# First chunk loaded in four-token runs over two hardware queues, scaled and turned by groups of heads, its layers taken batch by batch

The kernel runs on one core of one Trainium2 chip. The metric is the device time of the core in microseconds (us), as a median of the fast runs; less is better. Faster or slower needs 2%, with a 95% interval that lies clear of it.

## The reference

```python
def _attn_ref(q, k, v, alpha):            # each (4, 8, 768, 48): batch, head, token, dimension
    state = zeros((B, H, D, D)); y = zeros_like(q)
    for t in range(S):
        state = alpha[:, :, t, :, None] * state + einsum('bhd,bhe->bhde', k[:, :, t], v[:, :, t])
        y[:, :, t] = einsum('bhd,bhde->bhe', q[:, :, t], state)
    return y

def _moe_ref(x, w_in, w_out):             # x (3072, 384), w_in (384, 2048), w_out (2048, 384)
    h = x @ w_in
    c = sqrt(2.0 / pi)
    g = 0.5 * h * (1.0 + tanh(c * (h + 0.044715 * h * h * h)))
    return g @ w_out
# reference(): x is y with heads side by side, (4*768, 384); the result is _moe_ref(x)
```

So the work is linear attention with a decay per token, and then a feed-forward of two layers with a GELU between them. All of it is float32 at the borders.

## The kernel before

Time is cut into six chunks of 128 tokens. A chunk has two **pairs** of batches, so there are twelve pairs, 0 to 11. Pairs 0 and 1 are the first chunk, pair 2 is the first half of the second. For each pair ScalarE takes the logarithm of alpha, TensorE forms prefix sums over the tokens (a product with a triangle of ones), ScalarE takes two exponentials (of the sums and of their negatives), and VectorE scales q and k with them. TensorE turns q and k, multiplies them to scores, VectorE masks these, TensorE multiplies with v, and the result is copied and turned once more to be the input of layer 1. A state per batch is carried from chunk to chunk.

The order of the instructions on each engine is fixed when the kernel is built, by a list scheduler that works with guessed durations `W`. The loads of before run through one software queue, issued by GpSimd (POOL), but for the first alpha, which the SP queue takes:

```python
    DECAYS = {-1: (0, 1), 1: (2, 3), 2: (4,), ...}
    SPLIT = (2,)                       # pair 2 is loaded and scaled in two halves
    LOADS = ("0", "1", "in 0", "in 1", "in 2", "in 3", "out 0", "out 1", "out 2", "out 3",
             "2", "3", "4", "5", "6", "7", "8", "9", "10", "11")
    # "0" is alpha, q, k, v of pair 0; "in 0" the first quarter of w_in; "out 0" of w_out

    def load(self, n, c, i, lo=0, hi=2):          # tokens are the partitions: runs of 48 floats
    # ... cut: the tile; emit(e) opens ...
            src = self.src[n][2 * i + lo:2 * i + hi].rearrange("b h s d -> s (b h) d")[c * C:(c + 1) * C]
            (nc.sync if e == "SP" else nc.gpsimd).dma_start(u[n][:, lo:hi].rearrange("t b h d -> t (b h) d"), src)

    def fill(self, n):                            # "idle": products of zeros, meant to keep TensorE's clock up
    # ... cut ...
            for _ in range(n):
                self.nc.tensor.matmul(ps, self.zero[:, 0:self.C], self.zero, start=True, stop=True)
    # ... cut ...
        for m in range(len(self.BLOCKS)):         # the order of the layers: a block is a pair
            layer1(m)
            if m:
                for j in (0, 1) if m == 1 else (m,):
                    layer2(j)                     # block 0: quarter of w_out by quarter, over its two batches
```

Layer 2 of pairs 0 and 1 comes after layer 1 of both. Tile names in the profile: `a`, `la` alpha and its logarithm, `cum` prefix sums, `qp`, `kp` scaled q and k, `qkT` these turned, `at`, `atm` scores and masked scores, `yps` attention's output, `hT` layer 1, `gT` GELU, `acc` layer 2, `idle` the products of zeros.

## Time and profile before

| | before |
|---|---|
| time, median of 3 runs | 188.59 us (188.59 to 188.68) |
| span of the profiled run | 186.9 us |
| TensorE (PE) busy | 176.7 us, 95% |
| ScalarE (ACT) / VectorE (DVE) busy | 71% / 56% |
| products of zeros | 31, 11.2 us |
| share of the software queue, 16 DMA engines | 74.4% |

TensorE is busy nearly all the time, and where it is busy on zeros there is something to gain. That is only in the first 50 us, before it has a steady supply of work. The lines of the profile that show it are in the prediction below.

### The profile page before, as it was taken

To read this page: it belongs to the slowest core of one execution; us is meant where nothing else is said; L and a number is where in the kernel's file an instruction comes from. 1 tells how busy PE (TensorE), PEld (TensorE's weight loads), DVE (VectorE), ACT (ScalarE), POOL (GpSimd) and SP (SyncE) were. 2 spreads that over 40 slices of the span, in tenths; PEclk is the share of its full clock that TensorE was granted. 3 is DMA by queue.
4 is the path that set the end of the run, shared out by engine and by line. 5 is a ranking of instruction groups with operands and counts; after the bars stand their busy time and mean duration, and the time that the engine had idled before them with its cause. 6 is when DMAs were issued, how large, how long until landed. Compare 5 with 4: busy or idle time off the path is not lost.

```text
span 186.9 us, 4504 instructions
## 1 busy us (share of the span) xinstructions
PE 176.7 (95%) x1831; PEld 127.2 (68%) x1834; DVE 104.0 (56%) x219; ACT 131.8 (71%) x297; POOL 63.8 (34%) x67
## 2 busy tenths in 40 slices
PE   5788899999999999999999999999999999999990
PEld 1344688666687687687688778667687687786850
DVE  7268670079787597497499798696644615000000
ACT  2544889853769769859799759788789884582911
POOL 7993443796456575566552200000000000000000
PEclk9999999999999999999999999999999999999999
DMA  6999999999999999999999997153270280301111
GB/s 131 174 183 169 206 204 212 200 178 229 240 217 186 151 227 205 175 231 200 180 218 222 186 207 136 43 123 76 46 178 22 49 190 14 101 15 47 42 42 44
DMA packets 49781, 27.56 MB, mean 147 GB/s; under 512 B 39744, under 2 KB 46400, under 8 KB 49760
## 3 DMA queue, kind: packets, MB, share of 16 engines
q0 software_dynamic: 32464, 19.27, 74.4%
q1 hardware_dynamic: 17296, 8.00, 17.5%
q8 instruction: 14, 0.23, 0.6%
q14 instruction: 7, 0.06, 0.1%
HBM read 25.17 MB, written 4.72 MB: 160 GB/s over the span
## 4 chain that ended last, share of the span: by engine, by line
PE 88%; ACT 4%; DVE 3%; DMA 2%; issue 1%
PE hT L400 34%; PE acc L414 34%; PE at L327 4%; PE qkT_ps L291 4%; PE cum L254 3%; PE yps L376 2%; DMA a<-in_alpha_dram 2%; PE yps L373 2%; PE kv L344 2%; PE idle L209 2%; PE xT_ps L390 1%; DVE atm L334 1%; ACT qkT L305 1%; PE cum L256 1%; DVE qp L280 1%
## 5 line engine op out<-in xcount | busy, mean ns | idle before, releaser
L406 ACT ACTIVATE gT<-hT 128x256 bf16<-128x256 f32 x192 | 63.5, 386 | 11.0 <-PE hT L400 10.5
L400 PE MATMUL hT<-xT,w_in 128*128 128x256 bf16 x576 | 69.9, 273 | 0.3 <-ACT gT L406 0.2
L414 PE MATMUL acc<-w_out,gT 128*128 128x384 bf16 x384 | 68.6, 326 | 0.0
L400 PEld LDWEIGHTS <-w_in 128*128 128x128 bf16 x576 | 54.2, 98 | 8.6 <-issue 0.8
L414 PEld LDWEIGHTS <-gT 128*128 128x128 bf16 x384 | 35.7, 97 | 20.4
L334 DVE TENSOR_TENSOR atm<-at,ut 128x512 bf16<-128x512 f32 x48 | 31.0, 686 | 13.8 <-PE at L327 12.9
L280 DVE TENSOR_TENSOR qp<-q,b 128x768 bf16<-128x768 f32 (+1 forms) x13 | 11.6, 892 | 19.0 <-ACT b L272 16.7
L421 ACT COPY ot<-acc 128x384 f32<-128x384 f32 x17 | 8.2, 480 | 18.7 <-PE acc L414 18.5
L222 POOL DMA_DIRECT2D k<-in_k_dram x13 | 14.5, 1113 | 12.3 <-DVE kp L280 6.0
L222 POOL DMA_DIRECT2D q<-in_q_dram x13 | 14.6, 1122 | 9.5 <-DMA q<-in_q_dram 3.0
L222 POOL DMA_DIRECT2D v<-in_v_dram x13 | 14.4, 1111 | 7.3 <-DMA a<-in_alpha_dram 2.7
L222 POOL DMA_DIRECT2D a<-in_alpha_dram x12 | 13.3, 1110 | 7.8 <-DMA k<-in_k_dram 1.9
L272 ACT ACTIVATE b<-cum 128x768 bf16<-128x768 f32 (+1 forms) x13 | 9.9, 762 | 7.7 <-PE cum L256 7.6
L243 ACT ACTIVATE la<-a 128x768 f16<-128x768 f32 (+1 forms) x13 | 10.2, 793 | 3.5 <-DMA a<-in_alpha_dram 3.3
L209 PE MATMUL idle<-zero 128*128 128x512 bf16 x31 | 11.2, 483 | 1.4 <-DVE zero L596 1.2
L361 DVE TENSOR_TENSOR st<-stmp,bend 64x192 bf16<-64x192 f32 x32 | 11.3, 353 | 1.7
L200 ACT ACT_TABLE_LOAD x9 | 11.5, 1283 | 0.9 <-PEq L629 0.7
L280 DVE TENSOR_TENSOR kp<-k,binv 128x768 bf16<-128x768 f32 (+1 forms) x15 | 11.7, 792 | 0.2 <-DMA k<-in_k_dram 0.2
L359 DVE TENSOR_TENSOR stmp<-kv,st 64x192 f32<-64x192 f32 x32 | 11.3, 352 | 0.9 <-PE kv L344 0.6
L406 ACT ACT_TABLE_LOAD x9 | 11.5, 1283 | 0.2
L305 DVE COPY qkT<-qkT_ps 128x1024 bf16<-128x1024 bf16 (+1 forms) x14 | 8.8, 649 | 4.7 <-PE qkT_ps L291 4.6
L383 DVE CAST x<-yps 128x384 bf16<-128x384 f32 x12 | 6.7, 556 | 7.6 <-PE yps L376 7.5
(43 smaller groups left out, 151.3 us busy)
## 6 DMA issues: line engine op xcount, KB each, us to landing
out_dram<-ot SPq DMA_DIRECT2D x24, 192.0 KB, 3.8
q<-in_q_dram POOLq DMA_DIRECT2D x11, 384.0 KB, 13.2
k<-in_k_dram POOLq DMA_DIRECT2D x11, 384.0 KB, 13.2
a<-in_alpha_dram POOLq DMA_DIRECT2D x10, 384.0 KB, 13.0
v<-in_v_dram POOLq DMA_DIRECT2D x11, 192.0 KB, 13.0
w_in<-in_moe_w_in_dram POOLq DMA_DIRECT2D x4, 384.0 KB, 11.8
w_out<-in_moe_w_out_dram POOLq DMA_DIRECT2D x4, 384.0 KB, 15.3
a<-in_alpha_dram SPq DMA_DIRECT2D x1, 384.0 KB, 4.2
```

Of the source, the lines that this page charges most:

```text
L200: nc.scalar.add_instruction(mybir.InstLoadActFuncSet(name=nc.get_next_instruction_name(), act_func_set_id=i, engine=mybir.EngineType.Activ ...
L209: self.nc.tensor.matmul(ps, self.zero[:, 0:self.C], self.zero, start=True, stop=True)
L222: (nc.sync if e == "SP" else nc.gpsimd).dma_start(u[n][:, lo:hi].rearrange("t b h d -> t (b h) d"), src)
L243: self.nc.scalar.activation(u["la"][:, lo:hi, :, 0:self.D], u["a"][:, lo:hi], AF.Ln)
L280: self.nc.vector.tensor_tensor(u[n + "p"][:, lo:hi, :, 0:self.D], u[n][:, lo:hi], u["b" if n == "q" else "binv"][:, lo:hi], op=ALU.mult)
L305: self.copy(e)(t, u.pop(("T_ps", i, which)))
L334: self.nc.vector.tensor_tensor(u["atm", i][:, o], u["at", i][:, o], self.ut[:, None, :].to_broadcast([self.C, self.H // 2, self.C]), op=AL ...
L359: nc.vector.tensor_tensor(s[ps], acc, old[ps, :, fs], op=ALU.add)
L361: nc.vector.tensor_tensor(new[ps, :, fs], acc, u["bend"][ps, i, :, None].to_broadcast([64, H // 2, D]), op=ALU.mult)
L400: self.nc.tensor.matmul(h, self.w_in[:, j, nt * self.C:(nt + 1) * self.C], self.xT[c][:, j, lo:hi].rearrange("p g t -> p (g t)"), start=j ...
L406: return lambda e: self.nc.scalar.activation(self.gT[c % self.NG][:, nt, lo * self.C:hi * self.C], f.pop(("h", c, lo, nt)), AF.Gelu_apprx_ ...
L414: self.nc.tensor.matmul(f["acc", c, b], self.gT[c % self.NG][:, nt, b * self.C:(b + 1) * self.C], self.w_out[:, nt, :], start=nt == 0, sto ...
```

## The change

The intent is to shorten that head. Alpha, q and k of the first chunk, all four batches, are loaded with four tokens to a partition (runs of 768 B in place of 192 B), over the SP and the ScalarE hardware queues. The other loads wait until that alpha has landed. Prefix sums, exponentials, scaling and turning of the first chunk go by groups of two heads over all four batches at once. Batches 0 and 1 go singly through layer 1, layer 2 of the first chunk goes batch by batch (before, pair 0's went quarter of `w_out` by quarter over its two batches), pair 2 is loaded ahead of `w_out`, and pair 2 is no longer split. Layer 1 of the whole chunk comes ahead of its layer 2, as before. The diff, cut to its core:

```diff
-    SPLIT = (2,)
-    LOADS = ("0", "1", "in 0", "in 1", "in 2", "in 3", "out 0", "out 1", "out 2", "out 3", "2", "3", ...)
+    SPLIT = ()
+    LOADS = ("v0","v1","in 0","in 1","in 2","in 3","2","out 0","out 1","out 2","out 3","3", ...)
+    R = 4
+    ON_ACT = (("a", 2), ("a", 3), ("q", 2), ("q", 3))
@@
+    def load_first(self, n, b):
+            src = self.src[n][b, :, 0:self.C].rearrange("h (j r) d -> j h (r d)", r=R)
+            dst = self.first[n].rearrange("(j b) h r d -> b j h (r d)", b=4)[b]
+            (self.nc.sync if e == "SP" else self.nc.scalar).dma_start(dst, src)
@@
+    def cum_first(self, g, p):
+            for r in range(R):
+                for s in range(R):
+                    nc.tensor.matmul(cum[:, r * n:(r + 1) * n], self.ut_blk[s > r], la[:, s, :, 0:D],
+                                     start=s == 0, stop=s == R - 1, skip_group_check=True)
@@
+        for r in "aqk":
+            for b in range(B):
+                load([(r, "first")], "ACT" if (r, b) in self.ON_ACT else "SP", ..., self.load_first(r, b))
+        load(["gate"], "POOL", 100, 0, lambda e: self.nc.gpsimd.tensor_copy(self.gate, self.first["a"][:, 0, 0, 0:1]))
+        loads["gate"][0].deps += loads["a", "first"]
@@ (four groups of two heads; scores of any batch need all eight turned products)
+        for p in range(4):
+            ln = s.add("ln", ..., self.ln_first(g, p), loads["a", "first"], LN_EXP)
+            cum = s.add("cum", ..., self.cum_first(g, p), [ln])
+            ... two exponentials, two products, two turns with their copies ...
@@
-        for m in range(len(self.BLOCKS)):
-            layer1(m)
-            if m:
-                for j in (0, 1) if m == 1 else (m,):
-                    layer2(j)
+        layer1(0, 0, 1)
+        layer1(0, 1, 2)
+        layer1(0, 2, 4)
+        decays(2)
+        layer2(0, 0, 2)
+        decays(3)
+        layer2(0, 2, 4)
+        ...
```

The first run of zeros is guessed anew as well: ten products of zeros start after the changed set-up, where before had six. Cut above, and part of the change all the same: other guessed durations in `W` (a quarter of a weight 2000 ns for 1850, for instance), five `ot` buffers for six, and other buffers for some of the scores. They too can change the order on the engines.

## The prediction

> **What bounds the kernel now.** I read the page first (busy shares, the slices, the chain that ended last), then the same chain in order of time, then the busy times of each engine in short windows, and last the waits of the queue that issues the loads.
>
> ```profile
> PE 176.7 (95%) x1831; PEld 127.2 (68%) x1834; DVE 104.0 (56%) x219; ACT 131.8 (71%) x297; POOL 63.8 (34%) x67
> PE   5788899999999999999999999999999999999990
> PE 88%; ACT 4%; DVE 3%; DMA 2%; issue 1%
> L209 PE MATMUL idle<-zero 128*128 128x512 bf16 x31 | 11.2, 483 | 1.4 <-DVE zero L596 1.2
> ```
>
> TensorE is the bound: 176.7 us busy of 186.9, and 88% of the chain that ended last. But 11.2 us of that busy time are the "idle" matmuls on zeros, which keep its clock up while it has nothing to do, and nearly all of them lie in the first five slices. So time can be gained only in the head, before TensorE has a steady diet. The chain in order of time says where the head ends:
>
> ```profile
> 0.74 4.18 DMA a<-in_alpha_dram
> 6.83 3.01 PE idle L209 x7
> 19.50 1.65 ACT qkT L305 x3
> 22.04 1.31 PE hT L400 x12
> 27.32 6.55 PE hT L400 x60
> 33.87 2.60 PE acc L414 x16
> 50.28 1.14 PE hT L400 x9
> ```
>
> The first column is the start in us, the second the length. Layer 1 of the first chunk starts at 22.04, its layer 2 at 33.87, and layer 1 of pair 2 (the second chunk's first half) at 50.28. I call this last moment **S**. After it TensorE runs through to 182.74 with one hole of 2.25 us, at 123.04 to 125.29 (output copy, table load, first GELU). So the time is S + 136.6 us (186.9 - 50.28), plus 1.7 us between span and median time (188.59 - 186.9): **time = S + 138.3**. The change is worth what it does to S.
>
> What feeds the head are the loads, one queue that never pauses:
>
> ```profile
> 15.16 0.74 POOL L235 DMA_DIRECT2D w_out<-in_moe_w_out_dram  x1 [0.82 <-DMA q<-in_q_dram]
> 17.31 0.74 POOL L235 DMA_DIRECT2D w_out<-in_moe_w_out_dram  x1 [1.41 <-DMA k<-in_k_dram]
> 18.64 0.74 POOL L235 DMA_DIRECT2D w_out<-in_moe_w_out_dram  x1 [0.59 <-DMA v<-in_v_dram]
> DMA to landing us min/median/max: 14.8/15.3/15.6
> ```
>
> The issuer waits until an earlier load has landed, so its waits are landing times: q of pair 1 at 15.1, k at 17.3, v at 18.6. A 384 KB strip of alpha, q or k thus takes 2.15 us of wire, a v strip 1.3. The last w_out quarter was issued at 18.64 and landed 15.6 us later, at 34.2, so the eight weight quarters took (34.2 - 18.6)/8 = 1.95 us each. Check: first alpha lands at 4.92; less 2.1 of wire, 2.8 us of start; 2.8 + 6 strips x 2.15 + 2 x 1.3 + 8 x 1.95 = 33.9, against 34.2 seen.
>
> **What the skill says.** The Trainium skill, "DMA: Bandwidth & Descriptors", section Specifications: runs under 512 B do not reach line rate. Agrees: the 192 B runs of alpha give 393 KB / 2.15 us = 183 GB/s, while output stores alone in the tail (1536 B runs) move 51 GB/s at a share of 0.16 and 40 at 0.11, 320 to 360 GB/s while busy. The same page, section Queues, rings and completion order: each engine takes turns between queues packet by packet; and its Rules for kernel authors: spreading loads over issuing engines saves only issue time. The trace fits: a 192 KB store lands in 1.9 us with the engines free, but 3.8 us in the median, as it shares with the loads. So two hardware queues are no second wire, and q and k will have to share with v and weights. "TensorE: Matmul & The Clock Gate", Part 1: TensorE runs at half clock until kept busy for about 3.4 us. Agrees in kind: the first six zero matmuls of 512 columns take 2.74 us (0.46 each), three at 10.21 only 0.81 (0.27 each).
>
> **The change, part by part.**
>
> *Loads in four-token runs.* Six strips of chunk 0 (alpha, q, k of both pairs) become twelve pieces of 192 KB with runs of 4 x 48 x 4 = 768 B. At some 340 GB/s (the stores) a piece takes 0.58 us, all twelve 7.0 us against 6 x 2.15 = 12.9. The wire is 5.9 us ahead from then on. Alpha of all four batches lands at 2.8 + 4 x 0.58 = 5.1, where before half of it landed at 4.92.
>
> *Order and gate.* v and weights are issued only once alpha has landed. q and k are on the wire meanwhile, so it does not run dry. v then competes with k. If the engines share evenly from about 7 us, k lands at 11 to 14 rather than at 9.8. The order is now v, w_in, pair 2, w_out: w_in ends at 2.8 + 7.0 + 2.6 + 7.8 = 20.2 (before 26.3), pair 2 at 20.2 + 3 x 2.15 + 1.3 = 28.0 (before about 43), w_out at 28.0 + 7.8 = **35.7**, later than before's 34.2.
>
> *Decay and scaling.* All four batches at once in four groups: per group a log (0.5 us at 128x384), twenty small matmuls (16 of 96 columns at 0.043 as in kv, 4 tiny at 0.02: 0.8 us), two exponentials (0.49 each), two products (0.55), two transposed copies (about 0.5). ScalarE has 4 x 1.5 = 6 us, VectorE 4.4, and 4 us of copies fall to either: 14.4 us over two engines, so 7.2 after alpha, 12.4 at best; with k at 11 and its 2.2 us of products and the last copy, about 14. TensorE gains 2.1 us of prefix sums (3.2 for 2 x 0.53) and 0.9 us for turning k back; both lie mostly in the idle head and replace zero matmuls.
>
> *First layer by single batches.* From 14: scores 0.35, two masks 1.3 (0.65 each), y 0.2, copy 0.48, transpose 0.2, copy 0.35, and some 0.1 between each: 3.6 us, so layer 1 starts at about **17.7** instead of 22.04. A single unit costs half a pair's columns (128x128 matmuls run at about 0.055, twice as many): layer 1 of the chunk stays 10.5 us. It then waits about 1 us for the last w_in quarter. With 3 us of the other batches' scores, y, and transposes beside it, it ends at about 32 (before 33.87).
>
> *Second layer.* It now goes batch by batch, so the first batch already needs all of w_out: it stalls at each quarter and finishes at 35.7 + 0.65 = 36.35, where without the wait it would have ended at 34.6. Three batches follow, 3 x 2.6 = 7.8 us. The attention of pair 2 needs the table switch after the last GELU: 32.4 + 1.3 + log 0.85 + prefix 0.5 + two exponentials 1.6 + products 1.9 = 38.5, so nearly all its TensorE work (transposes 0.9, scores 0.66, kv 0.35, y 0.75, turns 0.34) and pair 3's prefix 0.5 fall behind the stall: 3.5 us, of which I let 0.5 hide. S = 36.35 + 7.8 + 3.0 = **47.15**, 3.1 us earlier. Time = 47.15 + 138.3 = **185.5**, 1.7% faster.
>
> After S nothing is changed in kind: pairs 2 to 11 are loaded, scaled and turned as before. The wire, 5.9 us ahead, stays ahead of a TensorE that is 3 us ahead (a pair costs 7.75 us of wire and about 13.4 of TensorE).
>
> **Rivals.**
> (a) *The load order gives it back.* If pieces run no faster than strips (1.07 us each), w_out lands at 41.6 and S is 53: time 191. The stores' rate speaks against it; for a part of it, the sharing of three queues. With pieces at 0.75 us w_out lands at 37.7 and the time is 187.5.
> (b) *k is the late one.* If v and weights take half of the engines, k lands at 14 and layer 1 starts at 20.5. The work of TensorE from there to S is 10.5 + 10.4 + 3.7 (rest of chunk 0) + 4.2 = 28.8, less 0.7 done before: S = 48.6, time 186.9. The store's 3.8 against 1.9 us speaks for it.
> (c) *The whole lead reaches the end.* If layer 1 starts by 16 and ends by 30, pair 2's attention fills the wait for w_out, and the pieces come nearer the 403 GB/s that weights reach (786 KB read in 1.95 us), 0.49 us each: S = 44.5, time 182.8. The hole at 123 us may go too, for 2 us more, or another may come: the order on each engine is fixed from guessed durations.
>
> **Range and chances.** (a) in its mild form and (b) give 187 to 188, the main line 185.5, (c) 183 or a little less. Range 182.6 to 188.4. Two per cent lie at 184.9, just under the main line; so within 2% is likeliest, 0.57; faster 0.39; slower, which needs (a) in full, 0.04.
>
> **What would show it.** Right: alpha's last landing near 5.1; first layer-1 matmul between 16.5 and 19; a wait for w_out of 1 to 3 us in the first batch of layer 2; pair 2's layer 1 near 47; from there the same 136.6 us to the end, within 1.5. Wrong: k after 14 us (then b); pieces over 0.75 us (a); no wait for w_out and S under 45 (c); or S as foretold but new holes later, where scalar work and table loads sit between the layers.

## The result

| | before | after |
|---|---|---|
| median of the same rounds | 188.63 us (188.59 to 188.68, 4 runs) | 191.10 us (190.66 to 191.76, 4 runs) |
| ratio | | 1.0134, 95% interval 1.0103 to 1.0164 |
| granted clock (share of full speed that TensorE was allowed), profiled run | over 0.9 in every slice | 0.988, 0.8 in two slices |
| span of the profiled run | 186.9 us | 189.5 us |

All runs were fast ones. A ratio is the mean time of one kernel's runs over that of the other's of the same rounds, so it is not quite the ratio of the medians quoted beside it. Executions over 1.5% slower than the fastest of the same kernel are left out of the means. The change is 1.3% slower: within 2%, but outside the range that was predicted.

The page after, the lines that answer to those of before (busy time and share and instructions of each engine; the busy tenths of TensorE in 40 slices; its granted clock in tenths; the chain that ended last, by engine):

```profile
PE 177.6 (94%) x1948; PEld 131.8 (70%) x1948; DVE 105.6 (56%) x223; ACT 134.8 (71%) x305; POOL 55.7 (29%) x59
PE   7488799999999999999989999999998999999992
PEclk9889999999999999999999999999999999999998
PE 73%; DVE 12%; DMA 6%; ACT 5%; issue 2%; SPq 1%; DVEq 0%; ACTq 0%
```

TensorE is as busy as before, but it ends the chain for 73% of the span where it was 88%, and VectorE has grown from 3% to 12%. The second and third slices (4.7 to 14.2 us) have a lower granted clock. The chain in order of time (start, length, what):

```profile
1.54 5.22 DMA a_first<-in_alpha_dram
7.43 1.29 PE cum L259 x16
8.81 1.30 PE cum L259 x16
...
11.43 0.70 PE cum L259 x16
...
18.30 0.49 PE at L444 x8
18.82 3.04 DVE atm L461 x5
...
44.29 2.53 DVE atm L461 x4
...
51.21 0.88 DVE kp L394
52.13 0.87 PE qkT_ps L405 x12
53.00 0.66 PE hT L530 x6
```

Alpha lands at 6.76, four groups of prefix sums follow one another at 1.3 us down to 0.7, and scores do not start before 18.30. From 44.29 to 52.09 the chain runs through VectorE (masks, state steps, products of pair 3). The last line is S, layer 1 of pair 2: 53.00, where before had 50.28. TensorE's own lines, in its timeline (start, length, instruction, idle time before it and what ended that):

```profile
1.20 3.81 PE L224 MATMUL idle<-zero 128*128 128x512 bf16 x10 [1.20 <-DVE zero L805]
7.43 1.29 PE L259 MATMUL cum<-la,ut_blk 128*128 128x96 f16 x16 [2.43 <-ACT la L246]
11.29 0.84 PE L259 MATMUL cum<-la,ut_blk 128*128 128x96 f16 x16
22.23 0.83 PE L530 MATMUL hT<-xT,w_in 128*128 128x128 bf16 x12
35.80 2.11 PE L549 MATMUL acc<-w_out,gT 128*128 128x384 bf16 x12
```

Layer 1 starts at 22.23 and layer 2 at 35.80. Three stages add up to S, and they say where the 2.7 us went and where the prediction went wrong:

| stage, us | before | predicted | after | after less before | after less predicted |
|---|---|---|---|---|---|
| start of layer 1 | 22.04 | 17.7 | 22.23 | +0.2 | **+4.5** |
| to the start of layer 2 | 11.83 | 14.3 | 13.57 | **+1.7** | -0.7 |
| from there to S | 16.41 | 15.15 | 17.20 | +0.8 | **+2.05** |
| S | 50.28 | 47.15 | 53.00 | +2.7 | +5.85 |
| S to the end of the span | 136.6 | 136.6 | 136.5 | -0.1 | -0.1 |

(The predicted stages are the prediction's own moments: 17.7, "ends at about 32", 47.15. Those of before are moments of the chain, as the prediction has them; in the timeline the first products of the layers are at 21.88 and 33.70, so product against product layer 1 starts 0.35 later than before, not 0.2.) The last row holds, but three things offset one another in it. Pair 3's turns, 0.87 us of TensorE's work, stand just behind S in before (at 51.43) and just ahead of it in after (at 52.13). The tail behind TensorE's last product is 0.6 us shorter (3.6 for 4.2). And TensorE idles for 1.6 us between S and its last product, where before had 0.2. The longest idle times there, in before and then two in after (TensorE's timeline; idle time and what ended it in brackets):

```profile
125.29 1.14 PE L400 MATMUL hT<-xT,w_in 128*128 128x256 bf16 x9 [0.17 <-ACT gT L406]
```

```profile
98.85 1.14 PE L530 MATMUL hT<-xT,w_in 128*128 128x256 bf16 x9 [0.69 <-ACT gT L539]
144.82 0.40 PE L444 MATMUL at<-qkT 64*128 64x128 bf16 x8 [0.59 <-DMA qkT<-kp]
```

So the "hole of 2.25 us" of the prediction, 123.04 to 125.29, was no hole: the chain leaves TensorE there, but TensorE has other products for all but 0.17 us of it.

Two further readings. The last quarter of `w_out` is issued at 23.3 and lands some 15 us later, at 38.4 rather than the predicted 35.7 (the line on `w_out` in the view of its loads):

```profile
DMA to landing us min/median/max: 15.0/15.1/15.5
```

And TensorE waits for only 0.3 us from layer 2's start to S (16.89 us busy of 17.20, zeros included). The groups of TensorE's work in that stretch (line, tile, shapes, count, then busy us and mean ns) differ in one thing that matters. Before, pair 2 alone is turned there (the row of k; that of q is like it):

```profile
L291 PE MATMUL qkT_ps<-ident,kp 128*128 128x128 bf16 x8 | 0.8, 219 | 0.0
```

After, pair 3 is turned there too, twice as many products; in the chain these are the 0.87 us just ahead of S:

```profile
L405 PE MATMUL qkT_ps<-ident,kp 128*128 128x128 bf16 x16 | 1.6, 220 | 0.1
```

### The profile page after: what moved, and what is told of

It is laid out like the page before. It is cut to its first block, busy times and chain, and to the rows that moved or that the text cites. A ratio compares the mean times of both kernels' runs of the same rounds, so it can differ in the third digit from the quotient of the medians.

```text
span 189.5 us, 4750 instructions
## 1 busy us (share of the span) xinstructions
PE 177.6 (94%) x1948; PEld 131.8 (70%) x1948; DVE 105.6 (56%) x223; ACT 134.8 (71%) x305; POOL 55.7 (29%) x59
## 4 chain that ended last, share of the span: by engine, by line
PE 73%; DVE 12%; DMA 6%; ACT 5%; issue 2%; SPq 1%; DVEq 0%; ACTq 0%
PE acc L549 28%; PE hT L530 25%; DVE atm L461 5%; PE at L444 4%; DMA qkT<-kp 3%; ACT gT L539 3%; DMA a_first<-in_alpha_dram 3%; PE qkT_ps L405 3%; PE cum L259 2%; PE yps L504 2%; PE yps L501 2%; PE cum L368 2%; DVE stmp L487 1%; PE kv L471 1%; PE xT_ps L518 1%
## 5 line engine op out<-in xcount | busy, mean ns | idle before, releaser
L530 PE MATMUL hT<-xT,w_in 128*128 128x256 bf16 (+1 forms) x624 | 70.2, 264 | 1.2 <-ACT gT L539 0.7
L549 PEld LDWEIGHTS <-gT 128*128 128x128 bf16 x384 | 35.7, 97 | 20.4
L327 POOL DMA_DIRECT2D v<-in_v_dram x12 | 13.9, 1162 | 15.9 <-PE xT_ps L518 8.4
L327 POOL DMA_DIRECT2D q<-in_q_dram x10 | 11.5, 1154 | 15.2 <-DVE qp L394 10.5
L394 DVE TENSOR_TENSOR qp<-q,b 128x768 bf16<-128x768 f32 x10 | 9.5, 955 | 7.6 <-ACT b L386 7.5
L327 POOL DMA_DIRECT2D a<-in_alpha_dram x10 | 11.5, 1154 | 5.9 <-DMA a<-in_alpha_dram 1.7
L327 POOL DMA_DIRECT2D k<-in_k_dram x10 | 11.5, 1152 | 4.7 <-DVE stmp L487 1.6
L511 ACT CAST x<-yps 128x384 bf16<-128x384 f32 x15 | 7.1, 476 | 5.5 <-PE yps L504 3.9
L444 PE MATMUL at<-qkT 64*128 64x128 bf16 x192 | 9.3, 219 | 1.3 <-DMA qkT<-kp 0.6
L444 PEld LDWEIGHTS <-qkT 64*128 64x128 bf16 x192 | 5.4, 94 | 7.0 <-issue 2.7
L386 ACT ACTIVATE b<-cum 128x768 bf16<-128x768 f32 x10 | 8.1, 811 | 2.9 <-PE cum L370 2.8
L419 DVE COPY qkT<-qkT_ps 128x1024 bf16<-128x1024 bf16 x12 | 7.7, 686 | 3.3 <-PE qkT_ps L405 3.3
```

The costliest lines, as they stand in the source:

```text
L386: self.nc.scalar.activation(u[n].rearrange("t i h d -> t i (h d)")[:, lo:hi], u["cum"][:, lo:hi, 0:H * D], AF.Exp, scale=1.0 if n == "b" e ...
L394: self.nc.vector.tensor_tensor(u[n + "p"][:, lo:hi, :, 0:self.D], u[n][:, lo:hi], u["b" if n == "q" else "binv"][:, lo:hi], op=ALU.mult)
L444: nc.tensor.matmul(at[o][:, p, :], k, q, start=True, stop=True)
L511: self.copy(e)(x, u["y", i].rearrange("t h d -> t (h d)"))
L530: self.nc.tensor.matmul(h[:, i * n:(i + 1) * n], self.w_in[:, j, nt * self.C:(nt + 1) * self.C], self.xT[c][:, j, lo:hi].rearrange("p g t ...
L549: self.nc.tensor.matmul(f["acc", c, b], self.gT[c % self.NG][:, nt, b * self.C:(b + 1) * self.C], self.w_out[:, nt, :], start=nt == 0, sto ...
```

## The experiments

My theory: the head did not get shorter. Alpha lands late, TensorE runs its prefix sums at half clock after 2.4 us of idling, and the grouping by heads keeps every batch waiting for all eight turned products; so layer 1 starts no sooner and then carries more work. The rivals: the order of loads or the gate costs the time; the single batches cost it; pair 2 being whole costs it; or the start of layer 1 does not set the end at all.

Below, "start" is the first layer-1 product and S is pair 2's layer 1, both of the profiled run. S is taken from the chain unless it is said otherwise. The profile of e7 fell in a slow run, so it is not used.

### e1_warm: keep TensorE warm until the prefix sums

```diff
-                    f = Task("fill", {"PE": n * W["fill"]}, 0, self.fill(n))
+                    f = Task("fill", {"PE": n * W["fill"]}, 0, self.fill(n + 5 * (free[e] == W["begin"])))
```

Fifteen products of zeros in place of ten; the order of all else is the same.

> Edit: fifteen instead of ten zero matmuls before the first prefix sum (so TensorE is busy until about 7.2 us instead of 5.0), same order otherwise. Theory A (the head is late because TensorE cools while it waits for alpha, and because alpha is late): the three slow groups of prefix sums take 0.8 us each instead of 1.3, layer 1 starts near 20.7 instead of 22.2, pair 2's layer 1 (S) near 52 instead of 53.0, time about 190.0. Theory B (only the late w_out holds the end of the head): S and time unchanged, 191.1.

Measured: 190.21 us (189.95 to 190.94, 6 runs) beside 188.79 of before, ratio 1.0065 (1.0048 to 1.0082). TensorE's timeline:

```profile
1.19 6.01 PE L224 MATMUL idle<-zero 128*128 128x512 bf16 x15 [1.19 <-DVE zero L805]
8.07 0.84 PE L259 MATMUL cum<-la,ut_blk 128*128 128x96 f16 x16 [0.87 <-ACT la L246]
```

Each group of prefix sums takes 0.84, not 1.29, and the second starts 0.78 after the first. In the windows of after (stretch, length, then busy us and count of PE, PEld, DVE, ACT, POOL, granted clock, DMA share, GB/s) the clock was halved in exactly that stretch:

```profile
8.00:11.00 3.00, 3.00 (x47) 3.00 (x45) 0.80 (x2) 2.26 (x6) 3.00 (x4) 0.50 1.49 276
```

In e1 it is full there, and 74 products go through where 47 did:

```profile
8.00:11.00 3.00, 2.93 (x74) 2.92 (x74) 0.86 (x2) 3.00 (x9) 2.90 (x3) 1.00 1.12 242
```

From the start of alpha's logarithm to layer 1 it took 13.9 us (7.50 to 21.36), against 15.4 in after (6.86 to 22.23). So the cold clock cost some 1.5 us of the head, and 0.9 us of the time by the medians, 1.3 by the ratios: between a third and a half of the 2.5 us of loss. Something else remains. In this profile, of the slowest of the six runs, layer 1 starts 0.9 us sooner than in after, and S only 0.4 (52.61).

### e2_q_behind: all q behind alpha on one queue

```diff
-    ON_ACT = (("a", 2), ("a", 3), ("q", 2), ("q", 3))
+    ON_ACT = (("a", 2), ("a", 3))
```

> Edit: all q pieces go behind alpha on the sync queue, the scalar queue carries only two alpha pieces. Theory A: the last alpha piece, which landed at 6.8 us because q shared the engines with it, lands near 5.3, everything gated by it moves 1.4 us: layer 1 starts near 20.8, the last w_out lands near 37.0 instead of 38.4, time about 189.6. If instead the late landing is the sync engine's own issue time (0.8 us a piece), alpha lands at 6.3 or later and the time stays within 0.5 of 191.1.

Measured: 190.41 us (189.80 to 191.24), ratio 1.0090 (1.0060 to 1.0121). Alpha's logarithm still starts at 6.8, so this profile does not show q on the ScalarE queue to be what makes alpha late. Start 22.15, S 52.38.

### e3_out_first: `w_out` ahead of pair 2, as before had it

```diff
-    LOADS = ("v0","v1","in 0","in 1","in 2","in 3","2","out 0","out 1","out 2","out 3","3", ...)
+    LOADS = ("v0","v1","in 0","in 1","in 2","in 3","out 0","out 1","out 2","out 3","2","3", ...)
```

> Edit: w_out is loaded before pair 2, as in the kernel before. Theory B (w_out after pair 2 holds layer 2): w_out has landed by 31, layer 2 starts without a wait, S near 51.3, time about 189.4. Theory A: the wait of 1.3 us for the last quarter goes, but the vector engine's chain of pair 2 and 3, which starts with the table switch after layer 1, sets S: at most 0.7 us gained, time 190.4 to 191.1.

Measured: 192.38 us (191.78 to 193.46), ratio 1.0198 (1.0159 to 1.0237). This profile was a warm one, with its start at 20.45 and layer 2 at 34.02, but S is at 52.73 all the same. Its chain:

```profile
25.22 16.84 DMA a<-in_alpha_dram
42.09 0.85 ACT la L357
...
52.73 0.65 PE hT L530 x6
```

With `w_out` first, an alpha of the second chunk that is needed ahead of S lands only at 42.06 and takes the lead away. The time is no better than that of after (the intervals overlap by a hair), so it is not the new order of loads that gives the gain back.

### e4_no_gate: the other loads not held until alpha has landed

```diff
-        load(["gate"], "POOL", 100, 0, lambda e: self.nc.gpsimd.tensor_copy(self.gate, self.first["a"][:, 0, 0, 0:1]))
+        load(["gate"], "POOL", 100, 0, lambda e: None)
```

> Edit: v and the weights are issued at once instead of after alpha, same order on every engine. If the gate helps (the change's intent): alpha lands at 7.5 us or later instead of 6.8, as v competes, layer 1 starts later, time 191.5 to 192.5. If the gate costs (it lets the wire run dry): w_in and w_out land 1 to 3 us earlier, time 189 to 190.5.

Measured: 191.16 us (190.70 to 191.24), ratio 1.0122 (1.0107 to 1.0137). Alpha's logarithm starts at 7.23 rather than 6.86, which lies within what other profiles of kernels with the gate show (6.3 to 7.5); the time is that of after. The gate is neutral for the end, and what it brings alpha is not shown.

This profile also limits the theory of the cold clock. After ten products of zeros TensorE idled for 2.16 us, and yet all prefix sums ran at 0.84 us. With the same ten, e5 idled for 1.88 us and lost the clock from the second group on, as did e2 (2.02); e6 (2.83), like after (2.43), had half clock from the first group; e3 (1.53) and e10 (0.78) kept it. So the idle time alone does not decide it, and the fifteen zeros of e1 and e8 are the cases in which it was kept by design.

### e5_split2: pair 2 in halves again

```diff
-    SPLIT = ()
+    SPLIT = (2,)
```

> Edit: pair 2 is loaded and worked in two halves again, as in the kernel before (one part of the change undone). Theory A2 (after layer 1's last GELU the vector engine's chain through pair 2, its products, copies, masks and state updates, sets S, not w_out): the first batch's chain is shorter by half a log, two half exponentials and two half products, S about 52 instead of 53.0, time about 190.2. Theory B (w_out and layer 2 on TensorE set S): unchanged at 191.1 within 0.5.

Measured: 190.61 us (189.44 to 191.24), ratio 1.0079 (1.0035 to 1.0123). Start 21.71, S 52.23. The interval overlaps that of after (1.0103 to 1.0164), so whether whole or split is better here is not decided; at most it is a part of the loss.

### e6_kv_after_y: pair 2's state products behind its output

```diff
-            kv = s.add("kv", {"PE": W["kv"]}, P + j, self.kv(u, j), [*ks, *loads["v", m, j]])
+            kv = s.add("kv", {"PE": W["kv"]}, P + j, self.kv(u, j), [*ks, *loads["v", m, j]] + ([y] if m == 2 else []))
```

This moves VectorE's state work (the `stmp` and `st` steps between 46.8 and 49.5 in the chain after) out of the way to S.

> Edit: pair 2's kv products are made to follow its y, so that kv does not hold the two PSUM buffers that y needs until the state update on the vector engine is done (3 us of state updates move behind the copies of x). Theory A2: S near 51 instead of 53.0, time about 189.0. Theory B: S held by TensorE's layer 2 after w_out, at least 52.5, time 190.6 or more.

Measured: 188.99, 189.79 and 191.47 us, ratio 1.0072 (1.0012 to 1.0132); a slow run at 192.45 is left out. S is at 52.4 in a profile whose start was a late 22.71. Inconclusive: the spread is as large as what was asked.

### e7_pairs: the first two batches as a pair through layer 1

```diff
-        layer1(0, 0, 1)
-        layer1(0, 1, 2)
+        layer1(0, 0, 2)
```

> Edit: layer 1 of the first pair in one go of 256 columns again, not batch by batch (one part undone). If single batches help, layer 1 starts 2 us later, near 24.3, and the time goes up by 1 to 2 us, to 192 to 193. If they do nothing for the end of layer 1, because the later batches' copies hold it anyway, the time is 191.1 within 0.5.

Measured: 191.71, 192.20 and 193.95 us, ratio 1.0206 (1.0150 to 1.0262); a slow run at 195.22 is left out. That is some 0.7% over after (1.0206 / 1.0134), though the two intervals overlap a little. So the single batches are probably worth having, and probably no cause of the loss.

### e8_warm_kv: e1 and e6 together

> Edit: fifteen zero matmuls as in the first experiment, and kv after y. If the head's late start and the vector engine's chain are separate losses, the gains add: 0.9 and about 2 us, time about 188.2, the same as the kernel before. If one hides the other, no better than the better of the two alone.

Measured: 190.09 us (189.91 to 191.42), ratio 1.0087 (1.0053 to 1.0122). The two do not add. In this profile (of the slowest run, 191.42) the head was both warm and early, with layer 1 at 20.16, 2.1 us sooner than in after, but S is at 51.92, only 1.1 sooner, and 0.4 of that is half of pair 3's turns, which stand behind S here. Its chain between is no longer TensorE's:

```profile
11.59 12.79 DMA w_in<-in_moe_w_in_dram
...
24.66 14.40 DMA w_out<-in_moe_w_out_dram
...
39.10 0.97 PE acc L549 x5
```

The last quarters of `w_in` and `w_out` land at 24.4 and 39.06, and layer 2 waits for the latter. The loads are a second bound, right behind the first, so repairs of the head reach S only in part (0.4 of 0.9 us in e1, about 1 of 2.1 here).

### e9_before_warm: the same cure on the kernel before

```diff
-                    f = Task("fill", {"PE": n * W["fill"]}, 0, self.fill(n))
+                    f = Task("fill", {"PE": n * W["fill"]}, 0, self.fill(n + 4 * (not free[e])))
```

Ten products of zeros in place of six, in **before**. It tests the root of the prediction, that an earlier layer 1 makes an earlier end.

> Edit to the kernel before, not the changed one: ten instead of six zero matmuls ahead of the first prefix sum, same order. If a cold TensorE costs wherever its work is on the head's path (theory A), the prefix sums of pair 0 take 0.3 us each group instead of 0.5, the seven zero matmuls behind them 1.5 us instead of 3.2, the first transposes start near 8.7 instead of 9.6 and layer 1 up to 0.9 us earlier: time 187.7 to 188.4. If layer 1's start in this kernel is set by loads (k and v of pair 1, w_in), nothing moves: 188.6 within 0.2.

Measured: 188.64 us (188.51 to 188.70) beside 188.71, ratio 0.9996 (0.9983 to 1.0008). Layer 1 starts at 20.86 instead of 21.88 (the first product; its place in the chain was 22.04), layer 2 at 32.87 instead of 33.70, and S is where it was:

```profile
28.55 10.70 DMA a<-in_alpha_dram
39.27 0.53 ACT la L243
...
50.25 1.14 PE hT L400 x9
```

The second half of pair 2's alpha lands at 39.2 in both kernels. In the unchanged one TensorE's work was just as late, so the chain ran through TensorE and hid the load behind it. The microsecond off the head of before was therefore worth nothing, and the chain puts it down to this load; e11 moves it.

### e10_alpha_alone: q and k held until alpha has landed

On top of e2: GpSimd writes one element of the q and k tiles from alpha, after the fourth alpha load, so that q and k are issued only then.

```diff
+            if n == "a":
+                self.held = getattr(self, "held", 0) + 1
+                if self.held == self.B:
+                    for x in "qk":
+                        self.nc.gpsimd.tensor_copy(self.first[x][:, 0, 0, 0:1], self.first["a"][:, 0, 0, 0:1])
```

> Edit to the changed kernel: all q and k pieces go on the sync queue and are held until alpha has landed (one element of each is written from alpha first), so alpha has the engines to itself. If sharing with q and k is what makes alpha late, it lands near 5.2 us instead of 6.8 (786 KB at some 340 GB/s after 2.8 us); q and k then land 2 us later, and the time is 190.5 to 192. If alpha lands at 6.3 or later all the same, its own issues and runs are what is slow.

Measured: 196.00 us (195.63 to 197.30), ratio 1.0372 (1.0357 to 1.0388), slower. Alpha alone on the wire lands at 5.74, a microsecond sooner than the 6.76 with q and k behind it, and sooner than in any other profile. Its last packets are moved at about 5.4 here; in after, the packets of the SP queue, counted in order, put the end of its alpha at about 5.6 (my estimate), so most of the difference lies between the last bytes and the landing. But q and k now stand against the software queue:

```profile
8.83 3.02 SPq L234 DMA_DIRECT2D qk_first<-in_k_dram  x4
...
19.69 1.03 DVE L285 TENSOR_TENSOR kp<-qk_first,binv 128x384 bf16<-128x384 f32 x2 [2.41 <-DMA qk_first<-in_k_dram]
...
28.42 0.83 PE L535 MATMUL hT<-xT,w_in 128*128 128x128 bf16 x12
```

q, issued from 6.1, lands at 13.1, and k, issued from 8.8, at about 19.6. This is the prediction's rival (b), made on purpose. Layer 1 starts at 28.42 (6.3 later than in e2), S is at 58.64 (6.3 later), and the median is 5.6 us longer; the granted clock, 0.965 to 0.974, was also below e2's 0.990 to 1.000. So in this family of kernels a later layer 1 does reach the end, nearly whole.

### e11_mix: from before, pair 2 ahead of half of `w_out`, and layer 2 by quarters over four batches

On top of e9:

```diff
-    LOADS = (..., "out 0", "out 1", "out 2", "out 3", "2", "3", ...)
+    LOADS = (..., "out 0", "out 1", "2", "out 2", "out 3", "3", ...)
@@
-        def layer2(m):
+        def layer2(*ms):
-            units = [(pairs[p][0], 2 * pairs[p][1] + j) for p in self.BLOCKS[m] for j in range(2)]
+            m = ms[0]
+            units = [(pairs[p][0], 2 * pairs[p][1] + j) for x in ms for p in self.BLOCKS[x] for j in range(2)]
@@
-                          gs[m][4 * part:4 * part + 4] + [loads["w", "out", part]], stream=n)
+                          gs[2 * u[0] + u[1] // 2][4 * part:4 * part + 4] + [loads["w", "out", part]], stream=n)
@@
-                for j in (0, 1) if m == 1 else (m,):
-                    layer2(j)
+                layer2(*((0, 1) if m == 1 else (m,)))
```

If the load at 39.2 held before, then bringing it forward while a late `w_out` is needed only quarter by quarter should make a kernel that is faster than both.

> Edit to the kernel before, with the ten zero matmuls: pair 2's loads are put between the second and third quarter of w_out, and layer 2 of the first chunk takes its four batches quarter by quarter, so that the last w_out quarters are needed late. If the kernel before is held at the end of its head by the landing of pair 2's second alpha half (39.2 us in both runs of it), this half lands near 35.5, S moves from 50.3 to about 49 and the time is 187.2 to 188.0. If TensorE's own work holds S there, the time stays at 188.6 within 0.3.

Measured: 187.72 us (187.57 to 187.94, 5 runs) beside 188.75, ratio 0.9947 (0.9934 to 0.9959). The chain:

```profile
24.78 11.01 DMA a<-in_alpha_dram
35.81 0.53 ACT la L243
...
49.17 1.14 PE hT L400 x9
```

The load lands at 35.8, 3.5 sooner, and S falls by 1.1, as the time falls by 1.0. The run has two edits besides e9's (the order of loads and that of layer 2), which only make sense together; that the landing alone does it is not shown.

### e12_mix_kv: e11 and pair 2's state products behind its output

```diff
-                    kv = s.add("kv", {"PE": W["kv"]}, P + 30 + j, self.kv(u, j), [k, loads["v", m, j]])
+                    kv = s.add("kv", {"PE": W["kv"]}, P + 30 + j, self.kv(u, j), [k, loads["v", m, j]] + ([y] if m == 2 else []))
```

> The same with pair 2's kv products after its y. If the state updates on the vector engine stand between the masks and the copies of x and set S in this kernel, a further 0.3 to 1 us, time 186.8 to 187.8; if they do not, equal to the run before it within 0.3.

Measured: 187.59 us (187.48 to 187.66), ratio 0.9938 (0.9925 to 0.9952). It beats both kernels, before by 0.6%, but it is not told apart from e11. In its profile the first product of pair 2's layer 1 is at 48.81 (timeline), 0.4 sooner than in e11, and the span is 0.3 shorter; the chain meets layer 1 only at 50.46, behind a table load and a GELU. Over all profiles the span less S is 136.3 to 137.7 us, so S plus a constant is a guide to about a microsecond.

## Why the prediction was wrong

The sum that was predicted, **time = S + 138.3**, held: 53.0 + 138.3 = 191.3, measured 191.1. That it held this well is luck: 0.87 us of work moved across S, 1.4 us of new idle time behind it and a tail shorter by 0.6 cancel. It is S that failed, by 5.85 us, in two of the three stages.

1. **"Layer 1 starts at about 17.7 instead of 22.04" was the step that failed most**: 22.23. Its terms:
   - "Alpha of all four batches lands at 5.1": 6.76, +1.7. The rate of the wire was near the 340 GB/s assumed (windows of 1 us from 3 to 8 us read 218 to 356 in after, 291 from 5 to 8). What was missing is the time from the last bytes to the landing: 0.4 us in e10, where alpha is alone (5.4 to 5.74), and about 1.1 in after, with q and k behind it (5.6, an estimate, to 6.76). In other profiles the logarithm starts anywhere from 6.3 to 7.5.
   - "0.8 us" for each group's prefix sums: 4.8 from the first to the end of the last, in place of 3.2, +1.6. This is the half clock that followed ten products of zeros and 2.4 us of idling in this profile; at full clock a group takes 0.84 (e1), so the 0.8 itself was right. I took the prefix sums as resting in an idle head, where zeros kept the clock up; the zeros ended at 5.0 and the sums began at 7.43. e1 shows that this was worth 0.9 to 1.3 us in the end; e3 and e4, with ten zeros, kept the clock, so in part it is chance from run to run.
   - The rest, about 1.2 us: a turned copy takes 0.68 on VectorE, not "about 0.5", and the first turn stands in TensorE's queue behind all four groups of prefix sums. The estimate "14.4 us over two engines" also took the work as freely divided, while the chain shows products, turns and copies one after the other. In the kernel before, pair by pair, the first mask starts at 12.87; in the changed one at 18.82, since it needs all eight groups. From the last turned copy to layer 1 it took about 3.7, against 3.6 foretold. That the grouping costs this is read from the chain; no run undoes it.
2. **Layer 1 itself, 14.3, was right** within 0.7: 13.57, without the full wait for `w_in`. It is 1.7 longer than before because the work of the other batches that before did ahead of it (their outputs, turns and state products) and the turning back of k, which is new, now lie beside it, and the single batches' share of layer 1 has waits for masks of some 0.4.
3. **From layer 2 to S, 15.15: failed**, 17.20. `w_out` landed at 38.4, not 35.7, but layer 2 began later too, and the first batch took 4.1 us with its wait (35.80 to 39.9; the stall was filled with prefix sums and zeros), against 4.35 counted. What failed is what follows: 13.1 us to S, against 10.8. Of these 2.3 us, 0.9 are pair 3's turns, which the scheduler put ahead of S (no lost time: before does them just behind S); 0.5 are the work that I let hide and that did not; the rest, some 0.9, is not pinned down: zeros and short waits, most of them just ahead of S, where the chain runs through VectorE for 7.8 us. Whether VectorE or TensorE's own order holds S there, e6 was to say, and it was inconclusive. Rival (a) foresaw S at 53 and a time of 191, the right numbers by luck, for a wrong reason: undoing the loads' order gains nothing (e3), and the pieces were fast, not slow.
4. **What no rival foresaw**: that in before the end did not hang on the start of layer 1 alone. By e9's chain a load landing at 39.2 held S at the same place. So the gains of a shorter head would have been real only together with the new order of loads, which the change does have; and with that order a later start of layer 1 reaches S whole (e10), an earlier one only in part (e1, e8), as `w_in` and `w_out` take over.

Of the rivals, (b) did not come about by itself: k was there by 13.0 at the latest (last issued at 6.8, at most 6.2 us to landing) and the product of k waits for no load. (c) hoped for 2 us from the hole at 123 us; TensorE idled for only 0.17 us in it, so there was nothing to gain, while "another may come" did come true, with 1.4 us of new idle time.

Left open: the greater part of the loss. The cold clock is the only cause that a run shows to cost time (0.9 to 1.3 us of 2.5). The grouping by heads, layer 2 batch by batch and the changed guesses and buffers were undone by no run, so each may hold a part. Also open: why the software queue's loads land some 2.7 to 3 us later than the sum of their pieces (`w_in` complete at 23.0 for 20.2, `w_out` 38.4 for 35.7) although the DMA engines hardly pause; and why alpha's landing varies by more than a microsecond from run to run. The spread of the changed kernel, 190.66 to 191.76, where before has 188.59 to 188.68, may come with it; the clock alone does not make it, since e1's six runs, all at 0.998 or more, still spread over 1.0 us.

## What to carry to other kernels

An earlier start of a stage is worth something only if nothing else holds the next one: before planning to shorten a head, look for the loads that land just ahead of the moment that matters, as they can hide behind a busy engine in the chain, and test with a cheap edit (here four more products of zeros) whether the start reaches the end at all. When work is regrouped so that many small steps serve all parts at once, count the path of the first part through all groups, not the sum of the work over the engines. And keep TensorE fed right up to the first real product: the zeros have to last until the data land, not until they were guessed to land.

## What the Trainium skill lacked or had wrong

- "TensorE: Matmul & The Clock Gate", Part 1, gives about 3.4 us of sustained work to warm up, at least one idle window of about 3.4 us to cool down, and says that the windows run freely. Here ten products of zeros, and then idling for less than that, were followed by half clock in four profiles (after 2.43 us, e2 2.02, e5 1.88, e6 2.83; in after granted 0.50 from 8 to 11 us and 1.29 us for 0.84) and by full clock in three (e3 1.53, e4 2.16, e10 0.78). That one kernel goes either way fits windows that run freely; what the page lacks is how much idling inside a window costs the clock. Fifteen zeros (5.7 to 6.0 us, with at most 0.9 us of idling) kept it in both profiles, e1 and e8. Whether TensorE cooled or had never quite warmed up, the trace doesn't tell: the granted clock reads 1.00 from 2 to 5 us, where the zeros still take about 0.38 us each, against 0.27 of warm ones in before.
- "DMA: Bandwidth & Descriptors", Queues, rings and completion order, says that engines take turns between queues packet by packet, but gives no measure of how loads on a hardware queue fare against a full software queue. Here 786 KB of q landed 7.0 us after the first was issued, and k some 11 us after (e10); issued ahead of the software loads, each piece of q and k landed 5.1 to 6.2 us after its issue (after). The same section gives no measure for a landing that is late with loads queued behind it: 6.76 against 5.74 us for the same bytes.
- No page gives a spread for the landing of the same first loads: alpha's logarithm starts at 6.3 to 7.5 us in the eight profiles of the changed kernel and its variants, e10 and the unused e7 aside.
